# Full-width q and k loads, two input-weight loads, filled gaps and a planner with a lock rule in an attention and gMLP kernel

## The chip, the cores and the metric

The kernel runs on one core of a Trainium2 chip. The time is the device time of one execution in microseconds (us). The engines are PE (matmuls), PEld (PE's weight loads), DVE (VectorE), ACT (ScalarE), POOL (GpSimd) and SP (SyncE), which here only issues transfers. Executions of the kernel before spread widely, so a run more than 1.5% above the fastest of its kernel counts as slow and is left out.

## The reference, cut to what matters

```python
q_n, k_n = rmsnorm(q, g_q), rmsnorm(k, g_k)          # 8 batches, 12 heads, 448 x 64, float32
attn = softmax(q_n @ k_n.T / sqrt(64))               # 448 x 448 per head
x = (attn @ v) -> (8, 448, 768)                      # heads side by side
h = maximum(x @ w_in, 0)                             # w_in 768 x 1024
u, v = h[..., :512], h[..., 512:]
v_n = (v - mean(v)) / sqrt(var(v) + 1e-6)            # layer norm of v
v_s = w_spatial @ v_n + b_spatial                    # over the 448 positions
out = (u * v_s) @ w_out                              # w_out 512 x 768
```

(Condensed from the numpy code; the arrow stands for the regrouping of heads. The kernel's matmuls are bf16.)

## The kernel before

One batch is three groups of four heads, so there are 24 groups. For a group, q and k arrive as one 448 KB tile each, are squared, reduced to 1/rms, scaled, turned (by PE for the first six groups, by a DMA transpose for the rest), and the turned k is multiplied by the product of both gains ("k scale"). Then come scores, exponentials, sums and values, and after each third group the gMLP part of that batch.

The program's order is not written by hand. Every piece of work is a task with the engines that may do it and, for each engine, how long it holds the engine and when its result is there. A planner simulates the engines with these lengths while the program is being built and emits, each time, the task that can start first. A wrong length costs nothing by itself, but it makes the order that the engines must keep.

```python
q_x = [q[b].rearrange("(x a g) (p s) d -> g x p a (s d)", x=2, a=2, s=NS) ...]
...
def emit(e, bf=bf, src=(q_x, k_x)[i][b][g]):
    for x in range(2):                                   # two transfers of 64 partitions
        sync.dma_start(out=bf.t[64 * x:64 * x + 64], in_=src[x])
raw_t[G, i] = add(f"load{i} G{G}", {"SP": (0.9, 0)}, due(G) - 26 + i * 0.1, emit, get=[bf], dma=1.65, ...)
...
dummies(40)                                              # matmuls that only warm PE, up front
...
for h, w, pos in ((1, w_in_v, 20.0), (0, w_in_u, 27.0)): # input weights: eight transfers
    for l in range(4):
        ... pool.dma_start(out=w[32 * l:32 * l + 32, :, :], in_=moe_w_in[192 * l:192 * l + 192, ...])
...
p = add(f"k_scale G{G}", {"DVE": (0.5, 0.6)}, d - 4, emit, ...)
...
dve.tensor_scalar(out=vn.t[0:n, c, :], in0=vs.t[0:n, c, :],   # layer-norm apply
                  scalar1=mv.t[0:n, c, 0:1], scalar2=rv.t[0:n, 1, c:c + 1],
                  op0=ALU.subtract, op1=ALU.mult)
```

(... marks cuts. GpSimd also multiplies: it squares and scales the tiles of the later groups, 128x896 at a time.)

## Time and profile before

| | before |
|---|---|
| time before the prediction, 3 runs | 312.76 us median (309.68 to 318.18) |
| profiled run | 318.62 us, span 316.8 us, mean granted PE clock 0.927 |
| first gMLP matmul of the first batch | 53.9 us |

The profiled run is in the upper part of that spread, above the 1.5% line, so its trace reads some 4 to 6 us longer than a middle run.

Three views carry what the prediction doesn't show. First the page of the profile: busy time by engine, the shares of the chain that ended last, and the issues of q and k loads (count, KB of each, median us from issue to landing).

```profile
PE 280.9 (89%) x2755; PEld 121.0 (38%) x2767; DVE 232.0 (73%) x356; ACT 215.8 (68%) x339; POOL 149.4 (47%) x128
...
PE 57%; DVE 15%; DMA 11%; ACT 7%; POOL 4%; issue 3%; SPq 1%; ACTq 0%; POOLq 0%; DVEq 0%
...
qf<-in_q_dram SPq DMA_DIRECT2D x48, 224.0 KB, 5.8
kf<-in_k_dram SPq DMA_DIRECT2D x48, 224.0 KB, 6.8
```

PE is the bound for most of the run, but a quarter of the chain is DVE and DMA. Next, two groups of DVE instructions (count, then busy us, mean ns): the k scale and the full-height layer-norm apply.

```profile
L444 DVE TENSOR_SCALAR kT<-kr,g_col 128x896 bf16<-128x896 bf16 x18 | 17.7, 984 | 3.6 <-DMA kr<-nk 3.6
L585 DVE TENSOR_SCALAR vn<-vs,mv,rv 128x512 bf16<-128x512 bf16 x24 | 15.8, 714 | 1.5 <-ACT rv L578 1.5
```

By the best times that the prediction gives, 434 and 395 ns, they take 2.3 and 1.8 times as long as they could. Third, SP's queue in the first 40 us (us in total, times, longest): it waits for earlier q and k loads to land before it may issue the next.

```profile
SPq L296 <- DMA qf<-in_q_dram: 3.9, 8, 0.9
SPq L296 <- DMA kf<-in_k_dram: 3.9, 8, 0.8
```

### The profile page before, as it was taken

What the parts mean: (1) busy time and instruction counts of PE and PEld (TensorE: products, weight loads), DVE (VectorE), ACT (ScalarE), POOL (GpSimd) and SP (SyncE); (2) the same over time, 40 slices, a digit from 0 to 9 for tenths busy, and PEclk for the clock granted to TensorE, in tenths of its full rate; (3) what the DMA queues carried; (4) which work ended last, traced back from release to release, by engine and by line L of the source; (5) the groups of instructions that cost most, each with busy time, mean ns of one, the idle gap of its engine ahead of it and who ended that gap; (6) DMA issues with size and microseconds to landing.
All of it is one profiled execution on the core that took longest, in us unless ns stands there. A gap on an engine that the chain in (4) does not pass through costs nothing.

```text
span 316.8 us, 6914 instructions
## 1 busy us (share of the span) xinstructions
PE 280.9 (89%) x2755; PEld 121.0 (38%) x2767; DVE 232.0 (73%) x356; ACT 215.8 (68%) x339; POOL 149.4 (47%) x128
## 2 busy tenths in 40 slices
PE   5168859999999699998997999998998899999993
PEld 5122424634444234343443434443433343444441
DVE  2791897988867957999897678778848756646563
ACT  3588596778788638696768787786876666874420
POOL 5532352432479808784997459929963200000000
PEclk9555597989999969999999999999999999999998
DMA  6999999807399964999999978999896342003205
GB/s 162 235 238 242 223 247 220 93 6 172 78 195 233 254 86 92 238 226 180 196 239 180 218 143 217 205 188 189 139 225 135 60 128 77 0 2 101 75 0 175
DMA packets 67466, 50.01 MB, mean 158 GB/s; under 512 B 42793, under 2 KB 64298, under 8 KB 67434
## 3 DMA queue, kind: packets, MB, share of 16 engines
q1 hardware_dynamic: 52354, 41.30, 60.8%
q0 software_dynamic: 15072, 8.27, 19.9%
q8 instruction: 21, 0.34, 0.5%
q14 instruction: 11, 0.09, 0.1%
q10 hardware_dynamic: 8, 0.00, 0.0%
HBM read 38.55 MB, written 11.01 MB: 156 GB/s over the span
## 4 chain that ended last, share of the span: by engine, by line
PE 57%; DVE 15%; DMA 11%; ACT 7%; POOL 4%; issue 3%; SPq 1%; ACTq 0%; POOLq 0%; DVEq 0%
PE ps L559 9%; PE ps L522 9%; PE ps L637 8%; PE pss L463 8%; PE ps L597 8%; PE ps L613 6%; PE ps L504 6%; DMA vt<-in_v_dram 5%; DVE vn L585 5%; DMA kr<-nk 4%; ACT et L486 4%; DVE kT L444 2%; DVE ms L387 2%; DMA qf<-in_q_dram 2%; DVE nq L401 2%
## 5 line engine op out<-in xcount | busy, mean ns | idle before, releaser
L486 ACT ACTIVATE et<-pss 128x896 bf16<-128x896 f32 x168 | 144.1, 915 | 23.7 <-PE pss L463 23.3
L463 PE MATMUL pss<-qT,kT 64*64 64x448 bf16 x672 | 54.2, 384 | 9.2 <-ACT et L486 7.6
L387 DVE TENSOR_REDUCE ms<-sq 128x14 f32<-128x896 f32 x48 | 51.4, 1075 | 3.9 <-ACT sq L377 2.6
L401 POOL TENSOR_TENSOR nk<-kf,rs 128x896 bf16<-128x896 f32 x21 | 37.4, 1782 | 23.6 <-ACT rs L394 14.8
L559 PE MATMUL ps<-w_in_v,xt 128*128 128x512 bf16 x180 | 45.5, 386 | 0.7
L522 PE MATMUL ps<-et,vt 128*32 128x448 bf16 x768 | 44.1, 370 | 0.8 <-DMA vt<-in_v_dram 0.8
L529 DVE TENSOR_TENSOR xt<-ps,rc 128x448 bf16<-128x448 f32 x48 | 29.3, 618 | 20.1 <-PE ps L522 15.9
L401 POOL TENSOR_TENSOR nq<-qf,rs 128x896 bf16<-128x896 f32 x16 | 27.2, 1701 | 32.9 <-ACT rs L394 28.8
L597 PE MATMUL ps<-xt,w_in_u 128*128 128x448 bf16 x192 | 39.6, 353 | 0.0
L379 POOL TENSOR_TENSOR sq<-kf 128x896 f32<-128x896 f32 x17 | 29.1, 1710 | 20.5 <-DVE ms L387 12.8
L637 PE MATMUL ps<-w_out,gt 128*128 128x384 bf16 x192 | 36.7, 328 | 2.1 <-DVE gt L618 2.1
L627 DVE COPY osb<-ps 128x384 f32<-128x384 f32 x51 | 27.9, 554 | 13.0 <-PE ps L637 9.6
L613 PE MATMUL ps<-w_spT,vn 128*128 128x448 bf16 (+1 forms) x128 | 29.7, 363 | 4.8 <-DVE vn L585 4.8
L463 PEld LDWEIGHTS <-kT 64*64 64x64 bf16 x672 | 14.5, 107 | 44.1 <-issue 41.2
L571 DVE BATCH_NORM_STATS2 s<-vs 128x6 f32<-128x512 bf16 (+1 forms) x32 | 22.0, 687 | 9.5 <-ACT vs L537 9.1
L379 POOL TENSOR_TENSOR sq<-qf 128x896 f32<-128x896 f32 x16 | 27.1, 1692 | 3.2 <-DMA qf<-in_q_dram 2.6
L618 DVE TENSOR_TENSOR gt<-ps,us 128x448 bf16<-128x448 f32 x32 | 19.6, 618 | 12.1 <-PE ps L613 9.4
L522 PEld LDWEIGHTS <-vt 128*32 128x32 bf16 x768 | 19.4, 100 | 23.7 <-issue 12.8
L312 POOL DMA_DIRECT2D vt<-in_v_dram x32 | 21.7, 688 | 11.3 <-DMA vt<-in_v_dram 10.8
L559 PEld LDWEIGHTS <-xt 128*128 128x128 bf16 x192 | 17.2, 99 | 25.2 <-issue 8.1
L504 PE MATMUL ps<-et,ones 128*32 128x448 bf16 x384 | 25.8, 395 | 0.0
L597 PEld LDWEIGHTS <-w_in_u 128*128 128x128 bf16 x192 | 17.3, 98 | 20.8 <-issue 6.5
(64 smaller groups left out, 260.8 us busy)
## 6 DMA issues: line engine op xcount, KB each, us to landing
qf<-in_q_dram SPq DMA_DIRECT2D x48, 224.0 KB, 5.8
kf<-in_k_dram SPq DMA_DIRECT2D x48, 224.0 KB, 6.8
out_dram<-osb SPq DMA_DIRECT2D x48, 192.0 KB, 3.2
vt<-in_v_dram POOLq DMA_DIRECT2D x16, 192.0 KB, 7.4
vt<-in_v_dram POOLq DMA_DIRECT2D x16, 144.0 KB, 8.2
out_dram<-osb SPq DMA_DIRECT2D x16, 96.0 KB, 4.2
w_in_v<-in_moe_w_in_dram POOLq DMA_DIRECT2D x4, 192.0 KB, 19.3
w_in_u<-in_moe_w_in_dram POOLq DMA_DIRECT2D x4, 192.0 KB, 12.2
```

Source lines behind the costliest of these rows:

```text
L379: eng_of[e].tensor_tensor(out=sqb.t, in0=r.t, in1=r.t, op=ALU.mult)
L387: dve.tensor_reduce(out=ms.t[:, i], in_=sqb.t.rearrange("p a (s d) -> p (a s) d", d=D), axis=AX.X, op=ALU.add)
L401: eng_of[e].tensor_tensor(out=nb.t.rearrange("p s a d -> p a s d"), in0=r.t.rearrange("p a (s d) -> p a s d", d=D), in1=P_rs[G % 4][:, i]. ...
L463: pe.matmul(out=ps[64 * h:64 * h + 64, a, 0:S], lhsT=kb[64 * a:64 * a + 64, slot, 64 * xk:64 * xk + 64], rhs=qb[64 * a:64 * a + 64, :, 64 ...
L486: act.activation(out=eb.t[:, r], in_=bf.t[:, :, 0:S], func=AF.Exp, bias=0.0, scale=1.0)
L504: pe.matmul(out=bf.t[32 * l:32 * l + 32, 0:S], lhsT=ones[:, (0 if c < 3 else 1 + x), :], rhs=eb.t[:, r, a, :], start=(c == 0), stop=(c == ...
L522: pe.matmul(out=bf.t[32 * l:32 * l + 32, 0:S], lhsT=vb.t[:, 3 * l + g, c, 32 * half:32 * half + 32], rhs=eb.t[:, r, a, :], start=(c == 0), ...
L529: dve.tensor_tensor(out=xb.t[:, j * S:j * S + S], in0=bf.t[:, 0:S], in1=rc.t, op=ALU.mult)
L559: pe.matmul(out=bf.t, lhsT=xb.t[:, j * S + 128 * c:j * S + 128 * c + 128], rhs=w_in_v[:, j, :], start=(j == 0), stop=(j == 5))
L597: pe.matmul(out=bf.t[:, 0:S], lhsT=w_in_u[:, j, 128 * f:128 * f + 128], rhs=xb.t[:, j * S:j * S + S], start=(j == 0), stop=(j == 5))
L613: pe.matmul(out=bf.t[:, 0:S], lhsT=vn.t[0:kp, c, 128 * f:128 * f + 128], rhs=w_spT[0:kp, c, :], start=(c == 0), stop=(c == 3))
L637: pe.matmul(out=bf.t[:, 0:384], lhsT=gt.t[:, f, 128 * c:128 * c + 128], rhs=w_out[:, f, 384 * h:384 * h + 384], start=(f == 0), stop=(f == 3))
```

## The change

The intent: fill the 128 partitions with one transfer per q or k tile; load the input weights in two transfers instead of eight; keep PE's clock up in the head with dummy matmuls in every planned gap; and give the planner lengths measured on the chip, the rule that GpSimd's operations and certain DVE operations exclude each other, and ScalarE as a second engine for the k scale.

```diff
-        at = max(free, t.after)
+        at = max(free[e], t.after)
+        if e == "POOL" or (e == "DVE" and t.port):
+            at = max(at, self.locked)
...
+            if (e == "POOL" and t.dma == 0) or (e == "DVE" and t.port):
+                self.locked = at + occ
             if t.dma:
-                dma = max(dma, at + occ + 1.3) + t.dma
-                t.done = dma + 0.7
+                dma = max(dma, at + occ + 1.6) + t.dma
+                t.done = dma + 1.3
...
-    dummies(40)
+    def fill(a, b):
+        if b < 25.5 and b - a > 0.6:
+            dummies(int((b - max(a, 2.0) - 0.4) / 0.11))
...
-    q_x = [q[b].rearrange("(x a g) (p s) d -> g x p a (s d)", x=2, a=2, s=NS) for b in range(B)]
+    q_x = [q[b].rearrange("(a g x) (p s) d -> g (x p) a (s d)", x=2, a=2, s=NS) for b in range(B)]
...
-                for x in range(2):
-                    sync.dma_start(out=bf.t[64 * x:64 * x + 64], in_=src[x])
-
-            raw_t[G, i] = add(f"load{i} G{G}", {"SP": (0.9, 0)}, due(G) - 26 + i * 0.1, emit, get=[bf], dma=1.65,
+                sync.dma_start(out=bf.t, in_=src)
+
+            raw_t[G, i] = add(f"load{i} G{G}", {"SP": (0.6, 0)}, due(G) - 26 + i * 0.1, emit, get=[bf], dma=1.4,
...
+    w_t = []
+    for a in range(2):
+        def emit(e, a=a):
+            pool.dma_start(
+                out=w_in[64 * a:64 * a + 64].rearrange("p (g h) f -> p g (h f)", h=2),
+                in_=moe_w_in[384 * a:384 * a + 384, :].rearrange("(g p h) f -> p g (h f)", g=NG, h=2))
...
-                    p = add(f"k_scale G{G}", {"DVE": (0.5, 0.6)}, d - 4, emit, deps=[p], get=[tb], use=[kr])
+                    p = add(f"k_scale G{G}", {"DVE": (0.38, 0.5), "ACT": (0.86, 0.96)}, d - 4, emit, port=True, deps=[p], get=[tb], use=[kr])
```

(Cut: some twenty other changed lengths; `port=True` at squares, scalings and the layer-norm apply; the head order in values, which follows from the new tile layout; the two small gain loads, which move from ACT to SP.)

## The prediction

> **What bounds the kernel now.** I read the page's slices first, to see where engines are idle and what the clock and the DMA do. Then I cut the run at the first gMLP matmul of each batch (line 559, first seen in the chain of waits at 54.37, 93.8, 130, 163.5, 196.6, 229.1, 263.5 and 294 us), because that interval is the kernel's real period. The slices:
>
> ```profile
> PE   5168859999999699998997999998998899999993
> PEclk9555597989999969999999999999999999999998
> DMA  6999999807399964999999978999896342003205
> GB/s 162 235 238 242 223 247 220 93 6 172 78 195 233 254 86 92 238 226 180 196 239 180 218 143 217 205 188 189 139 225 135 60 128 77 0 2 101 75 0 175
> ```
>
> A slice is 7.9 us. For the first seven the DMA engines are full but move only 223 to 247 GB/s, PE is partly idle and its clock is half for slices 2 to 5. From slice 8 on PE is nearly full at full clock, with a dip and a clock drop at slice 15. So there are two regimes, and the cut by period (times, busy of PE, PEld, DVE, ACT, POOL, clock, DMA share, GB/s) prices them:
>
> ```profile
> 0.00:54.40 54.40, 34.61 (x358) 17.37 (x360) 36.08 (x48) 35.02 (x52) 21.79 (x38) 0.69 1.11 224
> 54.40:93.80 39.40, 39.06 (x403) 17.64 (x405) 33.58 (x52) 30.77 (x50) 16.95 (x14) 0.96 0.62 108
> 93.80:130.00 36.20, 32.71 (x306) 12.83 (x307) 28.19 (x40) 24.39 (x40) 24.56 (x18) 0.91 0.88 170
> ...
> 229.10:263.50 34.40, 31.98 (x321) 13.08 (x323) 22.47 (x38) 24.29 (x37) 10.66 (x7) 1.00 0.65 128
> 263.50:294.00 30.50, 30.47 (x307) 12.60 (x308) 17.61 (x34) 20.10 (x29) 0.00 (x0) 1.00 0.18 47
> ```
>
> A head of 54.4 us, seven periods that sum to 239.6 (mean 34.2), and a tail of 22.8. The last period, 30.5, holds a whole gMLP and a whole attention like the others, but no GpSimd work and hardly any DMA: I take it as PE's own pace. So the waiting spread over the other six periods is 239.6 - 7 x 30.5 = 26 us, and the head is the largest single item.
>
> Why the head is long, from the chain of waits inside it and the waits by cause up to 54.4:
>
> ```profile
> 4.36 5.78 DMA qf<-in_q_dram
> 14.70 15.38 DMA vt<-in_v_dram
> POOL vt L312 <- DMA vt<-in_v_dram: 10.8, 3, 5.3
> POOL w_in_u L326 <- DMA w_in_v<-in_moe_w_in_dram: 5.3, 4, 1.7
> ACT et L486 <- PE pss L463: 5.7, 3, 3.1
> ```
>
> The order of cause is load, square, reduction, scaling, exponentials. The timeline has the squares of the first three q and k tiles at 5.64, 7.78, 10.23, 12.92, 14.84 and 16.75 us: each 448 KB tile takes 2.2 us on average, 209 GB/s. ACT stands in its queue for the next tile's square (10.23) before it may give the first group its 1/rms (11.42). The first scores start at 17.65 and the first exponential at 19.56. Then GpSimd stands 16.1 us on v and weight loads, and PE on v until 30.2.
>
> In the periods the loss is DVE's. Line 585 (layer-norm apply, bf16, SBUF to SBUF) takes 0.395 us at best and 1.79 at worst; 32 of them cost 23.1 us against 13 at the median 0.408. Line 444 (k scale) takes 0.434 at best, 3.0 at worst: 17.7 us against 7.8 for 18. The four of line 585 from 105.47 to 110.96 run beside GpSimd's multiplies of 1.7 us, PE waits for them, and the clock of slice 15 drops.
>
> **What the Trainium skill says.** (1) "SBUF — State Buffer", section on the DMA port swizzle: partitions 0 to 63 reach only 8 of the 16 DMA ports; 1 MiB was measured at 196 GB/s over 64 partitions and 328 over 128. The trace agrees with the low figure: 209 GB/s for tiles sent as two halves. (2) Same page, "Can I just issue two DMAs to hit both halves?": no, they serialize, +6% only. That is this kernel's load. The 128-partition rate is not in the trace, since no plain load here spans 128 partitions except w_out. (3) Same page, "Who interferes with whom": a DVE operation in a two-port mode and a GpSimd operation lock each other out for the whole instruction. The 0.4 against 1.8 us of line 585 agrees. (4) "TensorE: Matmul & The Clock Gate", Part 1: the array runs at half clock until about 3.4 us of sustained work and falls back after an idle window. Forty dummies warm it here, yet the trace shows 0.50 from 10 to 30 us.
>
> **The change part by part.**
>
> *One load over 128 partitions.* 48 fewer SP issues of 0.6 us, off the path. The gain is the rate: 2.2 us x 196/328 = 1.3 us per tile by the page's ratio; I take 1.5, an estimate, as v and weights share the engines. The sixth tile then lands about 4 us earlier and the first pair about 1.5. ACT no longer stands for the second group's tile before the first rstd. Chain after: k tile 6.2, square 0.95, reduce 1.08, rstd 0.55, scale 1.1 (twice on DVE or 1.7 on GpSimd), seven turns and two copies (about 2.3 in all): scores near 12.5 to 13. That is -5 us.
>
> *Input weights in two, v as before by strided heads.* Same bytes, but w_in goes from eight issues to two with 8 KB source runs and over 64 partitions instead of 32; GpSimd's 5.3 us behind w_in go, and most of the 10.8 behind v because these were queued among the pieces. PE waited 0.8 + 1.25 us for v with the exponentials idle 3.1 right after. About -3 us.
>
> *Dummies in every planned gap up to 25.5 us.* Between 17 and 38.5 us PE is busy 16.9 us at clock 0.50. Full clock would halve that, but only what lies before ACT counts: the sums and values of groups 0 and 1 (1.68 + 3.17 + two rounds of scores at 0.96, between which ACT idled). About -3.5 us. The dummies are in-order work, but 0.4 us is kept free of each gap.
>
> Head: 54.4 - 11.5 = 43.
>
> *Planner with the port lock, k scale allowed on ACT.* It changes only the order of instructions. Excess of DVE to be had: 10 us on line 585, 9.9 on line 444, 5.4 on the eight line 401 scalings (14.0 against 8 x 1.08). GpSimd keeps at least 64 operations of 1.7 us, so the locks cannot all be dodged. About half reaches PE: the chain gives line 585 4.8% (15 us) and line 444 2% (6.3 us). I take -1.5 us per period over seven, 10.5 of the 26 us. ACT, at 20 to 31 us of a period, takes some 0.86 us k scales without becoming the bound.
>
> *Strided weight columns for values (half::2).* The 32-column weight loads take 97 ns at the median and run beside matmuls of 353; even doubled they would mostly hide: 0.
>
> Sum for the profiled run: 43 + 7 x 32.7 + 22.8 = 294.7 against 316.8, ratio 0.930. On the 312.76 median: 291.
>
> **Rivals.** (a) *The head's gain is swallowed.* If groups 0 to 2 are paced by ACT (12 squares of 0.95 and 21 exponentials of 0.8 to 0.9, some 30 us from about 5) and later tiles, an earlier start yields only 5 us and the periods nothing: about 304 to 307. For it: ACT is busy 9.3 of 10 us at 20 to 30. Against: it is idle 3 to 5 of 10 at 10 to 20 and 30 to 40. (b) *The lock only moves.* A planner without lengths that hold puts the GpSimd work elsewhere, DVE keeps its 25 us of excess and the period stays 34: 300 to 302. For it: 106 us of GpSimd work is mandatory. (c) *More than I count.* If all periods reach 31, 43 + 217 + 23 = 283 on the trace, 279 on the median. For it: the last period shows PE can. Against: it had no transposes, locks or loads beside it. (d) *Dummies or moved k scales hurt*: dummies delay real matmuls when reality runs ahead of plan, at most a few us; alone they would not undo the rest.
>
> **Range and chances.** The head is the safer part (rate and clock are both seen in the trace), the period gain the less safe. Both rivals (a) and (b) end below 306.5, the 2% line, except at their worst together. The kernel before itself spreads from 309.68 to 318.18. Hence 291, range 279 to 303; faster 0.92, within 2% 0.06, slower 0.02.
>
> **What would show each step.** Loads: first squares spaced about 1.5 us and over 300 GB/s in some early slice. Start: first exponential at 14 to 15 us, not 19.56. Clock: slices 2 to 5 at 9. GpSimd waits on v and w_in below 5 us. First line 559 matmul near 43. Lock: line 585 mean under 0.55 us, from 0.72, and no slice 15 clock drop. Period near 32.7. I would be wrong if tiles still take 2 us (the rate is set elsewhere), if the clock stays half despite the dummies, or if PE stays full while the period does not shrink, so that its own mode switches were the pace.

## The result, and the profile after

| | before | after |
|---|---|---|
| median, 4 runs each in the same rounds | 314.03 us (309.68 to 318.18) | 293.88 us (293.45 to 295.06) |
| span of the profiled run | 316.8 us | 293.3 us |
| mean granted PE clock of that run | 0.927 | 0.984 |
| ratio of fast runs | 1 | 0.9449, 95% interval 0.9356 to 0.9541 |

The output is correct. The ratio is the mean time of one kernel's fast runs over that of the other's of the same rounds, so it isn't quite the ratio of the two medians. The medians differ by 20.15 us, but two of before's four runs (318.18 and 315.3) count as slow; the means of the fast runs, 311.22 and 294.06, differ by 17.2. The two traces differ by 23.5, because the profiled run of before was a slow one.

The page's slices after, 7.3 us each (PE busy and clock in tenths, GB/s moved):

```profile
PE   6568899998999999999999999999999999999992
PEclk9999898999999999999999999999999999999998
...
GB/s 238 318 291 241 297 227 106 31 209 91 188 240 260 163 122 213 272 212 188 212 182 223 206 161 176 217 201 190 236 202 57 75 191 2 0 2 121 70 0 189
```

The clock is 0.8 or more in every slice; the early half-clock stretch and the later dip are gone. The second slice moves 318 GB/s, where no slice of before reached 255. Cut at the first gMLP matmul of each batch, as in the prediction (us, busy PE, PEld, DVE, ACT, POOL, clock, DMA share, GB/s):

```profile
0.00:40.30 40.30, 29.68 (x413) 17.85 (x414) 33.35 (x47) 32.53 (x48) 14.93 (x30) 0.96 1.09 276
40.30:79.40 39.10, 37.21 (x393) 17.06 (x391) 31.54 (x49) 33.11 (x54) 19.33 (x13) 0.96 0.72 133
79.40:111.30 31.90, 31.37 (x321) 12.88 (x322) 22.55 (x38) 26.72 (x46) 25.21 (x18) 1.00 0.91 188
...
207.50:239.30 31.80, 31.75 (x333) 13.20 (x331) 20.43 (x34) 27.51 (x45) 14.28 (x12) 1.00 0.84 155
239.30:270.40 31.10, 31.00 (x313) 12.96 (x312) 15.64 (x30) 23.36 (x35) 0.00 (x0) 1.00 0.13 34
```

The head went from 54.4 to 40.3 us (14.1 less), the seven periods from 239.6 to 230.1 in sum (9.5 less), and the tail from 22.8 to 22.9. That is the 23.5 us. (The prediction's first cut lies 0.5 us behind before's real first matmul at 53.9; counted from there the head is 13.7 us shorter.) Inside the sum the first period stayed where it was (39.4 to 39.1) and the last too (30.5 to 31.1); the five between went from 169.7 to 159.9. In all five PE is busy for nearly the whole period now.

In the timeline of ACT's head (start, us, instruction, idle before it in brackets) the first squares are 1.2 and 1.65 us apart, and the first exponential starts at 14.44 us; before, that was 2.2 us on average and 19.56.

```profile
4.27 0.95 ACT L394 ACTIVATE sq<-qf 128x896 f32<-128x896 f32 x1 [2.24 <-DMA qf<-in_q_dram]
5.45 0.95 ACT L394 ACTIVATE sq<-kf 128x896 f32<-128x896 f32 x1 [0.23 <-DMA kf<-in_k_dram]
7.10 0.95 ACT L394 ACTIVATE sq<-qf 128x896 f32<-128x896 f32 x1 [0.70 <-DMA qf<-in_q_dram]
...
14.44 3.32 ACT L503 ACTIVATE et<-pss 128x896 bf16<-128x896 f32 x4
```

The page after:

```profile
PE 272.7 (93%) x2812; PEld 121.6 (41%) x2823; DVE 199.1 (68%) x324; ACT 232.5 (79%) x372; POOL 144.0 (49%) x121
...
PE 65%; DMA 9%; DVE 7%; issue 6%; ACT 5%; POOL 3%; SPq 3%; POOLq 0%; DVEq 0%; ACTq 0%
...
qf<-in_q_dram SPq DMA_DIRECT2D x24, 448.0 KB, 6.0
kf<-in_k_dram SPq DMA_DIRECT2D x24, 448.0 KB, 7.1
```

The share of DVE in the chain is halved. And look at the last two lines beside those of before: a transfer of twice the size lands after the same time. The groups of the layer-norm apply and the k scale after:

```profile
L602 DVE TENSOR_SCALAR vn<-vs,mv,rv 128x512 bf16<-128x512 bf16 x24 | 10.9, 508 | 1.8 <-ACT rv L595 1.8
L459 ACT ACTIVATE kT<-kr,g_col 128x896 bf16<-128x896 bf16 x9 | 9.4, 1043 | 0.6 <-DMA kr<-nk 0.6
L461 DVE TENSOR_SCALAR kT<-kr,g_col 128x896 bf16<-128x896 bf16 x9 | 7.3, 816 | 3.0 <-DMA kr<-nk 1.7 <-PE pss L480 1.3
```

The apply fell from 714 to 508 ns, and nothing on PE waits for it any more (before, PE's weight loads waited 7.0 us for it in seven places). Half of the k scales went to ACT.

### The profile page after: what moved, and what is told of

Its sections match the earlier page's. It is cut to its first block, busy times and chain, and to the rows that moved or that the text cites. A ratio compares the mean times of both kernels' runs of the same rounds, so it can differ in the third digit from the quotient of the medians.

```text
span 293.3 us, 6975 instructions
## 1 busy us (share of the span) xinstructions
PE 272.7 (93%) x2812; PEld 121.6 (41%) x2823; DVE 199.1 (68%) x324; ACT 232.5 (79%) x372; POOL 144.0 (49%) x121
## 4 chain that ended last, share of the span: by engine, by line
PE 65%; DMA 9%; DVE 7%; issue 6%; ACT 5%; POOL 3%; SPq 3%; POOLq 0%; DVEq 0%; ACTq 0%
PE ps L576 11%; PE ps L654 10%; PE pss L480 10%; PE ps L614 10%; PE ps L539 9%; PE ps L630 6%; PE ps L521 5%; DMA qf<-in_q_dram 4%; DMA kf<-in_k_dram 4%; ACT et L503 3%; PE ps L675 2%; DVE nk L418 1%; DVE nq L418 1%; POOL sq L396 1%; DVE ms L404 1%
## 5 line engine op out<-in xcount | busy, mean ns | idle before, releaser
L480 PE MATMUL pss<-qT,kT 64*64 64x448 bf16 x672 | 51.8, 366 | 6.7 <-ACT et L503 5.7
L418 POOL TENSOR_TENSOR nq<-qf,rs 128x896 bf16<-128x896 f32 x18 | 30.5, 1692 | 39.1 <-ACT rs L411 28.5
L576 PE MATMUL ps<-w_in,xt 128*128 128x512 bf16 x181 | 45.6, 387 | 0.7 <-issue 0.2
L539 PE MATMUL ps<-et,vt 128*32 128x448 bf16 x768 | 40.8, 354 | 0.0
L418 POOL TENSOR_TENSOR nk<-kf,rs 128x896 bf16<-128x896 f32 x17 | 29.9, 1761 | 21.3 <-ACT rs L411 21.3
L614 PE MATMUL ps<-xt,w_in 128*128 128x448 bf16 x192 | 39.8, 354 | 0.0
L644 DVE COPY osb<-ps 128x384 f32<-128x384 f32 x28 | 15.3, 555 | 16.8 <-PE ps L654 12.2
L614 PEld LDWEIGHTS <-w_in 128*128 128x128 bf16 x192 | 17.2, 98 | 20.8 <-issue 6.7
L654 PEld LDWEIGHTS <-gt 128*128 128x128 bf16 x192 | 16.7, 98 | 20.2 <-issue 7.2
L521 PE MATMUL ps<-et,ones 128*32 128x448 bf16 x384 | 23.3, 364 | 0.0
## 6 DMA issues: line engine op xcount, KB each, us to landing
w_out<-in_moe_w_out_dram POOLq DMA_DIRECT2D x1, 768.0 KB, 23.5
```

The lines of the kernel that those rows point to most:

```text
L418: eng_of[e].tensor_tensor(out=nb.t.rearrange("p s a d -> p a s d"), in0=r.t.rearrange("p a (s d) -> p a s d", d=D), in1=P_rs[G % 4][:, i]. ...
L480: pe.matmul(out=ps[64 * h:64 * h + 64, a, 0:S], lhsT=kb[64 * a:64 * a + 64, slot, 64 * xk:64 * xk + 64], rhs=qb[64 * a:64 * a + 64, :, 64 ...
L521: pe.matmul(out=bf.t[32 * l:32 * l + 32, 0:S], lhsT=ones[:, (0 if c < 3 else 1 + x), :], rhs=eb.t[:, r, a, :], start=(c == 0), stop=(c == ...
L539: pe.matmul(out=bf.t[32 * l:32 * l + 32, 0:S], lhsT=vb.t[:, 2 * (g + 3 * a) + x, c, half::2], rhs=eb.t[:, r, a, :], start=(c == 0), stop=( ...
L576: pe.matmul(out=bf.t, lhsT=xb.t[:, j * S + 128 * c:j * S + 128 * c + 128], rhs=w_in[:, j, DH:DF], start=(j == 0), stop=(j == 5))
L614: pe.matmul(out=bf.t[:, 0:S], lhsT=w_in[:, j, 128 * f:128 * f + 128], rhs=xb.t[:, j * S:j * S + S], start=(j == 0), stop=(j == 5))
```

## The experiments

The theory to be tested is the prediction's: loads gain by spanning 128 partitions, the dummies gain by the clock, two weight loads gain by freeing GpSimd's queue, and the lock rule gains by shorter DVE operations. The rival for each part is that the part does nothing and the gain comes from elsewhere; for the loads it is that the number of transfers counts and not the partitions. Each run is the changed kernel with the edit shown; e6, e8, e10 and e12 undo or change several things at once. All gave correct results. Times are medians; "over after" is the difference to 293.88 us, which crosses chips: e1 to e4 shared one, e5 to e8 a second, e9 to e11 a third, and e12 had a fourth. The ratios are to before on the run's own chip.

### e1: split each load by partitions

```diff
-                sync.dma_start(out=bf.t, in_=src)
+                for x in range(2):
+                    sync.dma_start(out=bf.t[64 * x:64 * x + 64], in_=src[64 * x:64 * x + 64])
```

> The changed kernel with each q or k load split again into two transfers over partitions 0 to 63 and 64 to 127; nothing else, and the same order of instructions. Theory (a transfer over 64 partitions is slow because it reaches only half of the ports): the first squares are spaced about 2 us again instead of 1.4, the first exponential starts 3 to 4 us later than 14.4 us, the first line 576 matmul at 46 to 50 us instead of 40.3, total 298 to 303 us. Rival (the head came from the new order, the clock and the GpSimd queue): first matmul within 2 us of 40.3, total 293 to 296.

Measured: 303.42 us (302.84 to 305.12), ratio 0.9727 (0.966 to 0.9793): 9.5 us over after. The first gMLP matmul is at 45.9 us instead of 40.3. From 2 to 10 us the core moves 216 GB/s, after 331. The time falls just above the theory's range and the first matmul just before it, and the first exponential comes at 20.70 us, 6.3 us later and not 3 to 4. That is later even than before's 19.56. One difference to before is that the two gain rows, now on SP's queue, take 1.3 us of its time between the second and the third tile; no run undid that move. So the way of loading is worth about half of the whole gain. But this edit changes two things, the partitions of a transfer and the number of transfers.

### e2: split each load, but over all 128 partitions

```diff
-                sync.dma_start(out=bf.t, in_=src)
+                for a in range(2):
+                    sync.dma_start(out=bf.t[:, a], in_=src[:, a])
```

> Each q or k load split into two transfers of the same 224 KB as in the run before it, but both over all 128 partitions (one head of the pair each). Port theory: as fast as the changed kernel, 293 to 295 us, first squares spaced about 1.4 us. Rival (what cost was the number and the size of the transfers: 224 KB each and twice the issues): as slow as the partition halves, 298 to 303.

Measured: 300.24 us (298.49 to 300.76), ratio 0.9606 (0.954 to 0.9672), beside e1 on the same chip: 6.4 us over after, 3.2 under e1. The first gMLP matmul is at 44.2 us, the early rate 235 GB/s. Every transfer spans 128 partitions, and two thirds of the loss is there all the same. The port explanation can hold for a third at most (e1 less e2), and even there a rival is left: SP takes 0.61 to 0.65 us to issue one of e1's halves and 0.42 to 0.43 for one of e2's (medians of the first 9 us). The rest goes with the number of transfers. SP's queue in the first 40 us shows one cost of it:

```profile
SPq L294 <- DMA kf<-in_k_dram: 9.3, 10, 2.8
SPq L294 <- DMA qf<-in_q_dram: 9.1, 9, 2.9
```

It waits 18.4 us for landings; the changed kernel waits for none there, only for buffers to come free. The program's own listing of SP's instructions (not a profile) tells why:

```
changed kernel                                          e2
 1 qf0  128x2x448                                     1, 2 qf0  128x448 x2
 2 kf0  128x2x448                                     3, 4 kf0  128x448 x2
 3, 4   the two gain rows                             5, 6 the two gain rows
 5 qf1  128x2x448                                     7, 8 qf1  128x448 x2
 ...                                                     9 kf1  128x448   waits DMAHW0
 8 kf2  128x2x448                                       10 kf1  128x448   waits DMAHW1
 9 qf3  128x2x448   waits DMAHW0                        11 qf2  128x448   waits DMAHW2
10 kf3  128x2x448   waits DMAHW1                        12 qf2  128x448   waits DMAHW3
```

(Copied with the names cut short; the numbers count transfers.) The program takes eight completion semaphores in turn, so the ninth transfer waits until the first has landed. At most eight are under way, whatever their size. Eight of 448 KB are 3.7 MB, eight of 224 KB half of that, and the landing takes 6 to 7 us either way.

These places can't be the whole of it, though. In e2 the first of SP's waits comes only after 9 us, and by then the third tile, which waits for no place, is late already: its square starts at 10.36 us instead of 7.10.

```profile
10.36 0.95 ACT L395 ACTIVATE sq<-qf 128x896 f32<-128x896 f32 x1 [2.94 <-DMA qf<-in_q_dram]
```

SP had issued it 1.3 us later than in the changed kernel (4.91 against 3.58), because each tile takes two issues. The rest of these 3.3 us is not explained.

### e3: the forty dummies up front again

```diff
-    plan.run(fill)
+    dummies(40)
+    plan.run()
```

> The changed kernel with 40 dummies up front and none later, as before the change; same order otherwise. Theory (warm clock is worth 3.5 us of head): clock near 0.5 from 10 to 30 us, first line 576 matmul at 43 to 44 us, total 296 to 298. Rival (with early loads the head is paced by ACT and DVE, which are busy 32.5 and 33.4 of 40.3 us, so PE at half clock fits beside them): the clock falls all the same, but total 293 to 295.

Measured: 295.55 us (294.12 to 296.38), ratio 0.9461 (0.9396 to 0.9525): 1.7 us over after, between the two forecasts, and first gMLP matmul at 41.7. The ranges of both kernels overlap, and by the ratios (0.9461 against 0.9449) the loss is 0.4 us: near the noise. The two windows from 10 to 26 us, first this run, then after:

```profile
10.00:26.00 16.00, 12.22 (x103) 5.87 (x107) 14.33 (x15) 12.70 (x19) 8.55 (x10) 0.50 1.16 282
```

```profile
10.00:26.00 16.00, 11.47 (x167) 6.72 (x168) 15.97 (x19) 14.40 (x23) 8.55 (x10) 1.00 1.16 282
```

The dummies do what they are for: the clock is 1.00 and not 0.50. But doubling it moves the first gMLP matmul by only 1.5 us. In the changed kernel DVE is busy 15.97 of these 16 us, so it seems that a faster PE just meets DVE; no run tested that.

### e4: input weights in eight pieces

```diff
+            src = moe_w_in[384 * a:384 * a + 384, :].rearrange("(g p h) f -> h p g f", g=NG, h=2)
+            for f in (1, 0):
+                for h in range(2):
+                    pool.dma_start(out=w_in[64 * a:64 * a + 64, h::2, DH * f:DH * f + DH],
+                                   in_=src[h][:, :, DH * f:DH * f + DH])
```

(in place of the one transfer of each half.)

> The changed kernel with its two input-weight loads issued as eight (2 KB source rows instead of 8 KB, each still over 64 partitions). Theory (GpSimd's 16 us of standing on v and weight loads came from the many small weight pieces): GpSimd waits again 5 us or more behind w_in or v, v and w_sp loads issue later, total 295 to 298. Rival (the waits came with the slow q and k loads that held the DMA engines, or GpSimd has slack in the head, where it now idles 19.4 us in one piece): no more than 1 us, 293 to 295.

Measured: 293.37 us (291.31 to 293.97), ratio 0.9378 (0.9294 to 0.9462): no slower than after. The first gMLP matmul is at 39.2 us. GpSimd's waits for transfers come back in the first 45 us, as these lines of its waits show:

```profile
POOL vt L331 <- DMA w_in<-in_moe_w_in_dram: 3.6, 3, 1.6
POOL w_in L346 <- DMA vt<-in_v_dram: 3.4, 2, 2.2
```

But they cost nothing: in the changed kernel GpSimd stands idle for 19.4 us in one piece there, waiting for ACT's 1/rms.

```profile
POOL nk L418 <- ACT rs L411: 19.4, 1, 19.4
```

So loading the weights in two is worth nothing that these runs can see. (Each piece of e4 still spans 64 partitions; the step from 32 to 64 was not undone.)

### e5: four transfers for each tile

```diff
+                for x in range(2):
+                    for a in range(2):
+                        sync.dma_start(out=bf.t[64 * x:64 * x + 64, a], in_=src[64 * x:64 * x + 64, a])
```

> The changed kernel with each q or k load split into four transfers of 112 KB (a partition half and one head each; same descriptors of 1,792 B). Theory now (only eight transfers of the SP queue may be under way, because the ninth waits for the completion semaphore of the first, so the bytes in flight set the rate): with 0.9 MB in flight the early rate of the q and k queue falls well below that of the halves (first squares spaced 3 us or more after the first group, against 2.0 to 2.5), the first line 576 matmul comes after 52 us, total above 312 us; SP waits for q and k landings grow beyond the 15 to 18 us that the halves showed. Rival (a fixed cost per issue of some 0.2 us, or the partitions): the step from halves to quarters is no larger than that from wholes to halves, total 300 to 308.

Measured: 316.2 us (315.78 to 316.96), ratio 1.0136 (1.008 to 1.0192): the loads alone eat the whole gain and more. First gMLP matmul at 52.9 us. The number is as the count theory has it, but the sign that I named for it failed: SP's waits for landings in the first 45 us did not grow; they are 3.9 and 1.4 us. SP's timeline (start, us) shows another limit:

```profile
0.74 2.50 SPq L295 DMA_DIRECT2D qf<-in_q_dram  x4
```

Issuing one tile takes SP 2.5 us (0.62 each), so on average tiles cannot come faster than that. The count of transfers has at least two costs: places among the eight, and SP's time to issue, which is 0.47 us for a whole tile over 128 partitions in the changed kernel.

### e6: the old lengths, no lock rule, k scale on DVE alone

```diff
-            if (e == "POOL" and t.dma == 0) or (e == "DVE" and t.port):
-                self.locked = at + occ
...
-                sw = 0.095
+                sw = 0.14 if t.mode == "S" else 0.1
...
-... {"DVE": (0.38, 0.5), "ACT": (0.86, 0.96)} ...
+... {"DVE": (0.5, 0.6)} ...
```

(and every other length as before; loads, dummies and weights stay new.)

> The changed kernel with the old planner: old lengths, no port lock, k scale on DVE only; loads over 128 partitions, dummies and weights as changed. Theory (the lock and the lengths are worth the rest of the gain, all of it in the periods): first line 576 matmul within 2 us of 40.3, mean period about 34 us instead of 32.9, DVE's layer-norm apply back at 0.65 us or more on average, total 300 to 304. Rival (the period fell because fewer and larger loads no longer hold up transposes and stores on the SP queue): total 293 to 297.

Measured: 301.66 us (299.06 to 302.44), ratio 0.9653 (0.9582 to 0.9723): 7.8 us over after. The first gMLP matmul is at 42.6 us, just outside the 2 us that the theory allowed, and the mean period 33.4 instead of 34, so over a third of the trace's loss is in the head after all. The apply is back at the level of before:

```profile
L600 DVE TENSOR_SCALAR vn<-vs,mv,rv 128x512 bf16<-128x512 bf16 x24 | 16.9, 755 | 1.5 <-ACT rv L593 1.5
```

### e7: the measured lengths without the lock rule

```diff
-            if (e == "POOL" and t.dma == 0) or (e == "DVE" and t.port):
-                self.locked = at + occ
```

> The changed kernel with the measured lengths but without the planner's rule that GpSimd and a DVE operation on the shared port exclude each other. If the lock rule is what matters: nearly as slow as with the whole old planner, 298 to 303, layer-norm apply 0.65 us or more. If the lengths are what matters: 293 to 296.

Measured: 312.29 us (308.9 to 313.28), ratio 0.9989 (0.9904 to 1.0073), on the chip of e6 and 10.6 us slower than it, outside both forecasts. So the measured lengths alone make the order worse than the old ones did. In the third period, three applies in a row on DVE:

```profile
137.24 5.14 DVE L600 TENSOR_SCALAR vn<-vs,mv,rv 128x512 bf16<-128x512 bf16 x3
```

and GpSimd in the same time:

```profile
137.03 1.83 POOL L416 TENSOR_TENSOR nk<-kf,rs 128x896 bf16<-128x896 f32 x1
138.83 1.72 POOL L394 TENSOR_TENSOR sq<-qf 128x896 f32<-128x896 f32 x1
140.51 1.72 POOL L394 TENSOR_TENSOR sq<-kf 128x896 f32<-128x896 f32 x1
```

One apply passes per GpSimd multiply: 5.14 / 3 = 1.71 us each, where the best is 0.4. Over the run the apply took 944 ns on average, and that period 40.5 us (32.5 in the changed kernel). Head and first period, 45.1 and 42.9, lose 8.6 us more.

### e8: spatial-weight turns as plain matmuls

The first period is the only one that did not shrink. The idea was that the 49 transposes of the spatial weights in it keep the clock down.

```diff
-                    pe.matmul(out=ps[64 * y:64 * y + 64, t, 0:64], lhsT=x, rhs=ident[0:64, 0:64],
-                              is_transpose=True, start=(t == 0), stop=(t == NS - 1))
+                    pe.matmul(out=ps[64 * y:64 * y + 64, t, 0:64], lhsT=x, rhs=ident[0:64, 0:64],
+                              start=True, stop=True)
```

(with the weights in eight as in e4.)

> A candidate: the changed kernel with the input weights in eight pieces, which came out 0.5 us faster, and the spatial-weight transposes as plain matmuls by the identity, so that the array's clock is not halved around 45 to 52 us. If transposes don't count as work for the clock, the first period (39.1 us) loses 1 to 2 us and the total is 291 to 292; if not, 293 to 294.

Measured: 294.06 us (292.83 to 295.25), ratio 0.9423 (0.9364 to 0.9483). The first period is 39.1 us again (39.0 to 78.15). But this doesn't clear the clock: from 48 to 52 us it is 0.61 in this run and 0.57 in the changed kernel, so the drop is still there. The form of the transposes is not what brings it. What the drop may cost is seen in the other runs. Where the clock over the first period is 0.96 (the changed kernel, e1 to e4, e8), the period takes 39.1 to 39.2 us; where it is 1.00 (e6, e10, e11, e12), it takes 37.2, 37.7, 36.8 and 36.8 us, for the same number of matmuls within three. In e11:

```profile
39.52:76.36 36.84, 35.91 (x395) 16.84 (x392) 32.31 (x50) 31.39 (x54) 20.30 (x15) 1.00 0.72 145
```

The same transposes run in e11 from 44.85 us, and no drop follows. What brings it stays open; and as the planned orders of these runs differ too, that the clock alone is worth the 2 us is likely but not shown.

### e9: a tiny transfer after each load

The full-size loads stay; only the number of transfers is that of e2.

```diff
                 sync.dma_start(out=bf.t, in_=src)
+                tiny = const.tile([16, 16], FP, name=f"tiny{len(tinies)}")
+                tinies.append(tiny)
+                sync.dma_start(out=tiny, in_=src[0:16, 0, 0:16])
```

> Each q and k load keeps its size (448 KB over 128 partitions), but a tiny transfer of 16 partitions by 64 bytes into a buffer of its own follows it on the same queue: as many transfers as with halves, with the bytes of the changed kernel. If only eight transfers are in flight on this queue, whatever their size (theory: the number of transfers is what halves cost), the tiny ones take half of the places: SyncE's queue waits for landings again in the first 40 us (10 us or more in all), the first gMLP matmul comes at 43 to 45 us and the time at 298 to 302. If the size of a transfer is what counts (rival: a 448 KB transfer runs better than one of 224 KB), the queue hardly waits, the first gMLP matmul stays within 1.2 us of 40.3 and the time is 293 to 296.

Measured: 299.69 us (297.46 to 301.55), ratio 0.9509 (0.9397 to 0.962): 5.8 us over after. (By the ratios it is only 1.9 us, as before was slower on this chip; but e11, on the same chip, has fast runs of 291.74 to 293.13, median 292.05, and e9 is 7.6 us over that, of which 2.3 are e11's shorter first period.) The first gMLP matmul is at 44.7 us, and SP waits for landings again, as the first theory had it:

```profile
SPq L297 <- DMA kf<-in_k_dram: 4.9, 2, 4.4
SPq L294 <- DMA qf<-in_q_dram: 4.2, 3, 2.2
SPq L294 <- DMA kf<-in_k_dram: 4.1, 3, 1.9
```

This is e2's loss with 1 KB added to each 448 KB. It is the count of transfers, not the size of one, that slows the head. What this run doesn't part is how much is places among the eight and how much is SP's issue time: each tiny transfer takes both (0.44 to 0.58 us to issue in the first 12 us).

### e10: the lock rule with the old lengths

The edits of e6 without the first one: the lock rule stays.

> The planner knows the lock of VectorE and GpSimd, but has the old lengths of operations and k scales on VectorE alone; loads, dummies and weights as in the changed kernel. If the lock rule is what counts: under 298, layer-norm apply under 0.6 us on average. If the rule is of use only together with the measured lengths (rival): 299 to 304, as without both (301.66), apply 0.7 us or more.

Measured: 298.79 us (297.25 to 301.06), ratio 0.9497 (0.94 to 0.9594): between both theories, which had under 298 and 299 or more. The apply fell to the level of after, as the first theory had it:

```profile
L602 DVE TENSOR_SCALAR vn<-vs,mv,rv 128x512 bf16<-128x512 bf16 x24 | 11.2, 518 | 1.4 <-ACT rv L595 1.4
```

### e11: k scale on DVE alone

```diff
-... {"DVE": (0.38, 0.5), "ACT": (0.86, 0.96)} ...
+... {"DVE": (0.38, 0.5)} ...
```

> The changed kernel with the k scales on VectorE alone again. If moving nine of them to ScalarE took a real load from VectorE (theory): 296 to 299, with PE waiting for the layer-norm apply or for k tiles. If VectorE has room (rival; it is busy 68% of the span): within 1.5 us of 293.9.

Measured: 292.59 us; the fast runs are 291.74 to 293.13 and one was slow, 297.4. Ratio 0.9285 (0.9196 to 0.9375). The median of the fast runs is 292.05, 1.8 us under the changed kernel and so a little better even than the rival had it. DVE has room, and moving nine k scales to ACT gained nothing here. Whether it cost something is not shown: the intervals of the ratios overlap, the chips differ, and this trace's first period is 2.3 us shorter, with the clock at 1.00 (see e8). The 18 k scales on DVE still took 818 ns on average, and nothing came of it.

This run also makes the clean comparison for e10. The two ran on one chip and differ in the lengths alone, both with the lock rule: 298.79 less 292.05, fast runs against fast runs, is 6.7 us for the lengths.

### e12: e4 and e11 together

> The two edits that each came out no slower than the changed kernel, together: k scales on VectorE alone, input weights in eight pieces. If their small gains are real and add: ratio to before 0.925 or less, 290 to 292 us. If they are noise between chips (rival, the likelier): ratio 0.93 to 0.945, 291.5 to 294.5 us, and the changed kernel stands as good as any of these.

Measured, five rounds: 292.09 us (fast runs 290.92 to 292.41), ratio 0.9359 (0.9301 to 0.9417). It falls into the band of the rival. Its interval overlaps that of after, and I did not run the two in the same rounds, so I don't claim a better version.

## Why the prediction was right

The prediction said 291 us, within 279 to 303, and faster with a chance of 0.92. The time is 293.88 us and faster. It was right on the number and on the shape: a head, periods and an unchanged tail. Some of its terms were right for another reason than the one given, and that the sum came out so near is partly luck: a weights term that is worth nothing and a dummies term twice too large stand against 4 us of the head that no term foresaw.

**One load over 128 partitions (-5 us): effect right, cause mostly wrong.** The first five squares come 1.39 us apart on average, against 1.5 assumed; the early rate is 331 GB/s and the first exponential is at 14.44 us, as foreseen. But the failing step is "The gain is the rate: 2.2 us x 196/328", with the half-partition ports as its reason, and "48 fewer SP issues of 0.6 us, off the path" beside it. Splitting over the same 128 partitions (e2) loses 6.4 us, and merely adding tiny transfers (e9) loses 5.8; only some 3 us at most are left for the partitions. The issues that I put off the path, with what comes behind each of them, are on it. In the program before, the second half of the fourth tile is already bound to the landing of the first tile's first half; in the trace SP stands for landings only after 9 us, 7.8 us in all by 40.

**Dummies (-3.5 us): mechanism right, size off.** The clock came up as predicted; the term measured 1.5 us of the head and 0.4 to 1.7 us of the time (e3). DVE was busy for all of that stretch, so the prediction's own rival, that ACT paces the head, seems to have had the right form with the wrong engine.

**Input weights in two (-3 us): wrong.** The waits of GpSimd fell away, as the prediction said they would, but putting them back (e4) costs nothing. The failing step is to turn GpSimd's 5.3 and 10.8 us of waiting into time of the path. Idle time of an engine that later stands idle 19.4 us in one piece was no loss.

**Head: 43 predicted, 40.3 measured.** The runs share the difference to before's 53.9 out as follows: 5.7 us for the loads (e1), 2.35 for the planner (e6, first gMLP matmul at 42.6), 1.5 for the dummies (e3). The remaining 4 us are not assigned. The profiled run of before was a slow one, and single undoings need not add up.

**Planner (-1.5 us per period): size right, its base misread.** The mean period fell from 34.2 to 32.9. (The prediction's cuts lie up to 1.3 us behind a batch's first matmul, as 163.5 for 162.2; the mean hardly changes.) But the prediction took 30.5 us as every period's floor and so found 26 us of waiting. Its own quoted line of the first period has 403 matmuls, where the last has 307; the extra ones are real work (turns of q and k by PE, and of the spatial weights), so 30.5 was out of reach there. Nothing was won in it: the whole 9.8 us came from the five middle periods, some 2 us each, so that seven times 1.5 came out right is luck too. But that PE is busy 39.06 of 39.40 us there does not mean that nothing was to be won: with the clock at 1.00, e6, e10, e11 and e12 needed 36.8 to 37.7 us for it (see e8). The prediction looked for the period's loss in DVE alone and did not price this clock.

**Lock rule and lengths.** The prediction treated the planner as one item. The four combinations, medians with the ratio to before of their own rounds:

| | no lock rule | lock rule |
|---|---|---|
| old lengths (k scale on DVE) | 301.66, 0.9653 (e6) | 298.79, 0.9497 (e10) |
| measured lengths | 312.29, 0.9989 (e7) | 292.05 (fast runs), 0.9285 (e11); 293.88, 0.9449 (changed kernel) |

With the rule, measured lengths are worth 6.7 us; without it they cost 10.6. Each pair is on one chip; the two k-scale options are too close to matter here (in e7 only one of 18 k scales went to ACT). A plan with tight lengths that doesn't know of the lock packs GpSimd's and DVE's work side by side, and e7's third period shows what becomes of it. How much of e7's loss is this and how much is chance of the order, one order cannot tell. The mean of the apply follows the rule first: 755 and 944 ns without it, 518 (e10), 404 (e11) and 508 (changed kernel) with it. The rule's effect on the time with old lengths is 2.9 us by the medians and 1.6% (about 5 us) by the ratios, across two chips, and the ranges of the two runs overlap.

**k scale on ACT: no gain** (e11). I had counted its 9.9 us of excess among what could be had. On ACT one took 1.04 us, not 0.86.

**Strided weight columns: 0**, as predicted as far as it shows. The weight loads of the values took 97 ns on average after and 100 before, so they did not get dearer. No run undid this part alone.

Undone one at a time, loads (9.5), planner (7.8) and dummies (1.7) give 19.0 of the 20.15 us between the medians; by the ratios, which set each run against before on its own chip, they give 8.7, 6.3 and 0.4, or 15.4 of 17.2 us.

**Still open:** why a landing takes 6 to 7 us for 224 KB as for 448 KB; how the cost of a transfer divides between issue time, the eight places and what makes the third tile late before any place is waited for; what moving the gain rows to SP's queue cost; and what brings the clock down near 48 us in the first period.

## What to carry to other kernels

When a load seems slow, count its transfers before its bytes or partitions: look at the issuing queue's own waits and issue times, and at how many transfers the program lets be under way at once. Before adding up waits as gain, ask whether the engine that waits, or the one that waits for it, is full in that stretch. And read the clock beside a full engine: PE busy 39.06 of 39.40 us looked like a floor, yet with the clock at 1.00 other orders needed 36.8 to 37.7. A planner's lengths and its exclusion rules belong together: accurate lengths with a missing rule came out worse than rough ones.

## What the Trainium skill lacked or had wrong

- "SBUF — State Buffer", section on the DMA port swizzle: its 196 against 328 GB/s led me to expect the gain from the partitions. (Its figures are for transfers of 1 MiB; these had 224 KB.) At an equal number of transfers, 64 against 128 partitions made 216 against 235 GB/s from 2 to 10 us and 252 against 281 from 10 to 40 (e1, e2), some 10%, and 3.2 us of the run, the difference in SP's issue times included.
- "DMA: Bandwidth & Descriptors", section "Rules for kernel authors", says not to bother with two transfers to disjoint partition halves and to use one of 128 partitions. The advice holds here (9.5 us, e1). But its reason, that the halves share the same engines, doesn't say that the second transfer itself costs something: two transfers over the full 128 partitions lose 6.4 us as well (e2), and a 1 KB transfer after each load loses 5.8 (e9).
- I found no page that has the limit which the program's listing shows: eight completion semaphores taken in turn by the transfers of SP's queue (in the program before, also by the two of ACT's), so that the ninth waits for the first (18.4 us of such waits in 40 us in e2, none in the changed kernel).
- I found none either with the issue times on SP by shape. Medians of the first 9 us: 0.47 us for 448 KB over 128 partitions (changed kernel), 0.43 for 224 KB over 128 (e2), 0.61 for 224 KB over 64 (before), 0.60 for 112 KB over 64 (e5).
